# One tile's feed-forward steps begin at the tenth of sixteen packing groups, on a new layout of PSUM

## The chip, the cores and the metric

The kernel runs on one core of one Trainium2 chip. A core has TensorE (PE, matmuls into the accumulator memory PSUM, eight banks), VectorE (DVE), ScalarE (ACT), GpSimd (POOL), and SyncE (SP), which here issues most of the loads. The metric is the device time of one execution in microseconds.

## What is computed

Everything is f32. Packing attention takes 32 learned vectors per head over the keys and values; a second attention lets each token look at its head's 32 packed vectors; then come a dense feed-forward layer and a layer in which each token goes to one of eight experts.

```python
p_packed = sm_attn(p, k, v)                 # 8 batches, 8 heads, 32 x 576
x = sm_attn(q, p_packed, p_packed)          # 576 tokens per batch, head width 64
h = x @ w_in                                # 4608 x 512 -> 2048
g = where(h >= 1, h, where(h <= -1, 0, (h + 1)**2 / 4))
x = g @ w_out                               # -> 512
e = argmax(x @ w_gate); out = gate * (relu(x @ w1[e]) @ w2[e])
```

The kernel splits an f32 operand into a high and a low part and takes three matmuls per product: high by high, high by low, low by high.

## The kernel before

The work is in three parts: a packing stage, 12 tiles of tokens with 16 steps each, and 18 slots of expert work with a tail. Only the first two touch the change.

**Packing** goes over 16 groups (a batch and four of its heads). For a group, four score matmuls go into two banks of PSUM (`sc`, L413); VectorE takes the maximum over 576 keys (`nm`, L420, L421); ScalarE takes the exponential into the group's K buffer `kp` (L423); TensorE transposes the result in five blocks (L431 four into `tp`, L433 the last into the bank of `av`); ScalarE copies them out (L434 to L436); twenty small matmuls with V (L446) give `av`, which ScalarE scales into `packed` (L447). The score pool has two buffers, so a group's score may run before the last group's exponential is done. Three K buffers and three V buffers go round; they are the places of later weight tiles (`pw03`, `pw13`, `wo7`, and `pw02`, `pw12`, `wo6`).

**Weight units.** Beside the groups run 16 units of weights (four for each n = 0 to 3; two of them first-layer halves g, two second-layer). `load_unit` (L292) brings 1 MB of 64-bit numbers into a raw buffer that the table `RAW` names; the last four go into K buffers and the buffer `wr`. `prep_unit` (L303) makes two f32 parts of it: Abs on ScalarE (L315), four operations on VectorE (L316 to L319), a cast on ScalarE (L320), a subtraction on VectorE (L321). First-layer units are multiplied by the packed vectors into the weights that tile 0 needs: `first_product` (L338), 12 matmuls of 512 columns per (n, g), two casts and two subtractions of 128x512 (L351, L352). `spill` (L323) writes the unit to DRAM for the other tile pairs, which make their products by `product` (L354): three matmuls for each of four k, with casts and subtractions over 64 partitions each.

**Tile 0's attention** is four chains (`attn_chain`, L229) of a query load (SyncE, L237) and three pieces, hung to iterations of the packing loop by `soon`; tile 0 is of kind M: 512 columns from two batches, two pieces of 256. **A step** (`step`, L1012) is for one of 16 slices of the hidden width: 12 matmuls of 256 columns (`h`, L718), the activation on ScalarE and VectorE (L740 to L748), and 12 matmuls of 512 columns (L723 to L725) that add the slice of the step before to four `y` tiles. After the sixteenth the four are copied out (`yr`, L775).

**Order.** The program is written by one loop over the groups. A scheduler moves the instructions of TensorE, ScalarE, VectorE and GpSimd by their dependencies; SyncE's stay as written. `LEAD` (3) is how many steps are written in the packing loop, `at` hangs work to later steps. PSUM before: `h`, `a0`, `a1`, `y0`, one bank each, and the score pool of four, which is closed after the last group and becomes a second `h`, `a2`, `y1`, `y2` (the pool `late`).

Of the kernel before, what the change touches and what calls it, by code (L numbers as in the profile page):

```python
# [23 lines left out]
P = 128  # L24
# [14 lines left out]
LEAD = 3  # L39
# [45 lines left out]
def attn_moe_kernel(ctx, tc, qT, kT, vv, pT, wcat, wg, w2cat, out):  # L85
# [91 lines left out]
    def h_tile(G, name):  # L177
        if late and G % 2 and G >= 10:
            return late[0].tile([P, 512], F32, name=name, tag="h")
        return psm.tile([P, 512], F32, name=name, tag="h")  # L180
# [10 lines left out]
    n_y = [0]  # L191

    def y_tile(name):


        i = n_y[0] % 3 if late else 0
        n_y[0] = i + 1
        return (late[0] if i else psm).tile([P, 512], F32, name=name, tag=f"y{i}")
# [30 lines left out]
    def attn_chain(col0, b, ws, n, g, ah, al, pl, sfx):  # L229
# [5 lines left out]
        def load():  # L235
            qr = pl.tile([P, 2, SPLIT + HB], F32, name="qr" + sfx, tag="qr", bufs=2)
# [37 lines left out]
    def tile_chains(t, pl):  # L274
# [4 lines left out]
        for pi, (col0, b, ws, n) in enumerate(tile_pieces(t)):  # L279
            for g in range(2):  # L280
                r.append(attn_chain(col0, b, ws, n, g, ah, al, pl, f"_{t}_{pi}_{g}"))
# [8 lines left out]
    RAW = ["wo4", "wo5", "wr"] * 4 + ["pw03", "pw13", "wo7", "wr"]  # L290
# [47 lines left out]
    def first_product(n, g):  # L338


        if g == 0:
            products(0, n)
        for par in range(2):
            ps = a_tile([P, 512], f"pp0_{n}_{g}_{par}")
# [9 lines left out]
    def product(p, n, k):  # L354

        if k == 0:
            products(p, n)
        g, q = divmod(k, 2)
        ps = a_tile([P, 512], f"pp{p}_{n}_{k}")
        for i, (t, m) in enumerate(((0, 0), (0, 1), (1, 0))):  # L360
            pe.matmul(ps, lhsT=both(k, t), rhs=ws1[0][:, q, m, :], start=(i == 0), stop=(i == 2))
# [10 lines left out]
    def packing():  # L372
        p1_cm = tc.tile_pool(name="st1p", bufs=2, space=PSUM)
        p1 = p1_cm.__enter__()
        if True:
# [51 lines left out]
            def s1_tr(i):  # L427
                s = d[i]
                ps = a_tile([P, 512], f"tp{i}")
                for c in range(4):  # L430
                    pe.transpose(ps[:, c * P:(c + 1) * P], s["a1"][:, c * P:(c + 1) * P], ident)  # L431
                s["ps"] = a_tile([P, 512], f"av{i}")
                pe.transpose(s["ps"][:64, 256:384], s["a1"][:, 512:], ident)  # L433
                act.copy(s["tA"], ps[:, :384])  # L434
                act.copy(s["tB"][:, :P], ps[:, 384:])
                act.copy(s["tB"][:64, P:], s["ps"][:64, 256:384])  # L436
# [37 lines left out]
            for c, (load, pieces) in enumerate(tile_chains(0, st2)):  # L474
                soon(3 + 2 * c, load)
                for m in range(3):
                    soon(5 + 2 * c + m, pieces[m])
            for i in range(NG + 2):
                if i < NG:
                    s1_score(i)  # L480
                    s1_exp(i)
                if i == NG - 1:
                    p1_cm.__exit__(None, None, None)
                    late.append(ctx.enter_context(tc.tile_pool(name="late", bufs=1, space=PSUM)))
                if 0 <= i - 1 < NG:
                    s1_av(i - 1)
                if i < NG:
                    s1_tr(i)
# [6 lines left out]
                for u in range(-(-NU * i // NG), min(-(-NU * (i + 1) // NG), NU)):  # L495
# [3 lines left out]
                    if u % 4 < 2:  # L499
                        todo.append((u // 4, u % 4))  # L500
                if i >= 5 and todo and todo[0][0] < 2:
                    first_product(*todo[0])
                    spill(*todo.pop(0))
                if i == NG - 1:
                    for u in range(NU, FC):
# [606 lines left out]
```

## Time and profile before

| | us |
|---|---|
| median of three runs | 1249.33 (1248.11 to 1250.98) |
| the profiled execution | 1249.28 |
| its span | 1247.3 |
| first maximum of the packing starts | 10.6 |
| sixteenth maximum starts | 113.6 |
| last first-product subtraction starts | 162.08 |
| tile 0's results start to be copied out | 196.38 |

The page lists each engine's busy time over the whole span, and the views below cut it into stretches. A row of an engine in order of time gives the start, the duration, the line, the operation, output and input, and in brackets how long the engine had stood idle before and what ended the wait. Matmuls overlap: the distance between starts is what one costs, not its duration.

### The profile page before, as it was taken

What the parts mean: (1) busy time and instruction counts of PE and PEld (TensorE: products, weight loads), DVE (VectorE), ACT (ScalarE), POOL (GpSimd) and SP (SyncE); (2) the same over time, 40 slices, a digit from 0 to 9 for tenths busy, and PEclk for the clock granted to TensorE, in tenths of its full rate; (3) what the DMA queues carried; (4) which work ended last, traced back from release to release, by engine and by line L of the source; (5) the groups of instructions that cost most, each with busy time, mean ns of one, the idle gap of its engine ahead of it and who ended that gap; (6) DMA issues with size and microseconds to landing.
All of it is one profiled execution on the core that took longest, in us unless ns stands there. A gap on an engine that the chain in (4) does not pass through costs nothing. (4 is left out here: it accounts for less than half of the span.)

```text
span 1247.3 us, 21251 instructions
## 1 busy us (share of the span) xinstructions
PE 1193.9 (96%) x7234; PEld 995.3 (80%) x7234; DVE 944.6 (76%) x2222; ACT 730.0 (59%) x1430; POOL 325.5 (26%) x567
## 2 busy tenths in 40 slices
PE   5787999999999999999999999999999999999997
PEld 2455888778778887678888887788999999999996
DVE  8888867988895959977869679899766666666663
ACT  4666656667566556565565455655565555555653
POOL 3221116623741105731211265512101000010010
PEclk8988999999999999999999999999999999999999
DMA  9995780143211232111331000601212512111150
GB/s 347 370 328 176 283 245 22 43 142 126 68 47 62 68 113 101 50 44 35 108 126 45 28 18 35 186 18 50 78 36 68 170 44 60 35 54 49 34 178 21
DMA packets 70179, 128.18 MB, mean 103 GB/s; under 512 B 10281, under 2 KB 46633, under 8 KB 66864
## 3 DMA queue, kind: packets, MB, share of 16 engines
q1 hardware_dynamic: 56464, 97.33, 24.2%
q0 software_dynamic: 5840, 18.95, 4.1%
q10 hardware_dynamic: 7760, 10.49, 2.7%
q8 instruction: 59, 0.97, 0.3%
q14 instruction: 56, 0.46, 0.1%
HBM read 162.31 MB, written 31.77 MB: 156 GB/s over the span
## 5 line engine op out<-in xcount | busy, mean ns | idle before, releaser
L718 PE MATMUL h<-ah,pw 128*128 128x256 f32 (+1 forms) x1024 | 242.6, 302 | 8.2 <-DVE rt L742 8.0
L869 DVE TENSOR_TENSOR sw<-raw,sw 128x1024 fp32r<-128x1024 f32 (+1 forms) x152 | 180.9, 1209 | 77.9 <-ACT sw L867 77.8
L885 PEld LDWEIGHTS gh<-gx,sw 128*128 128x128 f32 x1728 | 227.1, 191 | 12.8
L885 PE MATMUL gh<-gx,sw 128*128 128x256 f32 x1728 | 230.5, 283 | 0.0
L723 PE MATMUL y<-wo,gh 128*128 128x512 f32 x576 | 229.9, 399 | 0.6 <-ACT kp L423 0.6
L724 PE MATMUL y<-wo,gh 128*128 128x512 f32 x576 | 228.5, 397 | 0.0
L547 DVE CUSTOM_DVE_ANT_0 jk<-yr,wgb 128x512 bf16<-128x512 f32 x288 | 219.1, 761 | 5.6 <-ACT yr L775 3.5
L718 PEld LDWEIGHTS h<-ah,pw 128*128 128x128 f32 x1024 | 176.5, 190 | 31.0 <-DVE rt L742 13.4
L867 ACT CAST sw<-raw 128x1024 fp32r<-128x1024 f32 (+1 forms) x160 | 156.5, 1004 | 59.1 <-PE gy L725 53.9
L725 PE MATMUL y<-wo,gl 128*128 128x512 f32 x576 | 186.3, 400 | 2.1 <-POOL gl L748 1.9
L740 ACT ACTIVATE rt<-h,half 128x320 f32<-128x320 f32 (+1 forms) x192 | 111.0, 580 | 102.6 <-PE h L718 86.2
L747 ACT CAST gh<-rt 128x512 fp32r<-128x512 f32 (+2 forms) x192 | 98.1, 512 | 96.6 <-DVE rt L742 59.1
L718 PE MATMUL h<-al,pw 128*128 128x256 f32 (+1 forms) x512 | 152.7, 298 | 0.0
L742 DVE SCALAR_TENSOR_TENSOR rt<-h,rt 128x320 f32<-128x320 f32 (+1 forms) x192 | 105.5, 551 | 51.1 <-ACT rt L741 46.3
L908 POOL DMA_INDIRECT out<-go,xm x37 | 36.8, 993 | 362.3 <-ACT go L907 303.1
L725 PEld LDWEIGHTS y<-wo,gl 128*128 128x128 f32 x576 | 105.8, 189 | 30.0 <-POOL gl L748 5.1
L723 PEld LDWEIGHTS y<-wo,gh 128*128 128x128 f32 x576 | 108.7, 189 | 23.3 <-issue 2.1
L724 PEld LDWEIGHTS y<-wo,gh 128*128 128x128 f32 x576 | 108.9, 189 | 18.7
L889 ACT ACTIVATE ggh<-gh 128x256 fp32r<-128x256 f32 x144 | 55.0, 382 | 109.5 <-PE gh L885 103.8
L724 PE MATMUL gy<-sw,ggh 128*128 128x512 f32 x288 | 113.9, 395 | 0.0
L723 PE MATMUL gy<-sw,ggh 128*128 128x512 f32 x288 | 113.8, 395 | 0.0
L748 DVE TENSOR_TENSOR gl<-rt,gh 128x512 fp32r<-128x512 f32 (+1 forms) x128 | 84.1, 658 | 25.3 <-ACT gh L747 21.2
(220 smaller groups left out, 1762.5 us busy)
## 6 DMA issues: line engine op xcount, KB each, us to landing
raw<-in_w2cat SPq DMA_DIRECT2D x76, 1024.0 KB
ws<-wsd SPq DMA_DIRECT2D x48, 512.0 KB
wr<-in_wcat SPq DMA_DIRECT2D x16, 1024.0 KB
kp<-in_kT SPq DMA_DIRECT2D x16, 576.0 KB
xb<-xs SPq DMA_DIRECT2D x72, 128.0 KB
vr<-in_vv SPq DMA_DIRECT2D x16, 512.0 KB
wsd<-ws SPq DMA_DIRECT2D x8, 1024.0 KB
qr<-in_qT ACTq DMA_DIRECT2D x16, 320.0 KB
```

The costliest lines, as they stand in the source:

```text
L547: dve.tensor_tensor_reduce(out=junk, in0=rows[j][:, :DM], in1=wgb[0][:, e, :], scale=1.0, scalar=0.0, op0=ALU.mult, op1=ALU.add, accum_out ...
L718: pe.matmul(ps[:, col0:col0 + n], lhsT=w[:, g, part, c], rhs=x[:, g, col0:col0 + n], start=(n_mm == 0), stop=(n_mm == 5))
L723: pe.matmul(y, lhsT=gh, rhs=wh, start=first, stop=False)
L724: pe.matmul(y, lhsT=gh, rhs=wl, start=False, stop=False)
L725: pe.matmul(y, lhsT=gl, rhs=wh, start=False, stop=last)
L740: act.activation(v, ps[:, :W], AF.Relu, bias=half, scale=0.5)
L742: dve.scalar_tensor_tensor(out=v, in0=ps[:, :W], scalar=1.0, in1=v, op0=ALU.max, op1=ALU.min)
L747: act.copy(gh[:, :n], vk[:, :n])
L748: (pool if k == "A" else dve).tensor_tensor(out=gl[:, :n], in0=vk[:, :n], in1=f32(gh[:, :n]), op=ALU.subtract)
L867: act.copy(w[:, n, 0], r)
L869: (pool if sid == 0 and i else dve).tensor_tensor(out=w[:, n, 1], in0=r, in1=f32(w[:, n, 0]), op=ALU.subtract)
L885: pe.matmul(ps[:, :SL], lhsT=first(sid, 4 * (fc // 4) + k, part)[:, c], rhs=rh[:, k, :], start=(n_mm == 0), stop=(n_mm == 3 * KD - 1))
```

## The change

`LEAD` becomes `STEP0` = 9: a step is written at the end of every iteration from the tenth on, so nine of them lie in the packing loop's 18 iterations in place of three. To have room for four `y` tiles from then on, the main pool holds `h`, `a0`, `a1` and three `y`, the score pool has one buffer of two banks, and `late` is a second `h` and `a2`. A group's transposes and `av` share one bank (`bank(...)`, always the first from the eleventh group on), and the last transposed block goes into spare columns of the group's own score tile. The query loads of tile 0's second piece go into buffers of the steps' activation (`spare`), and its chains are hung to earlier iterations. First products for n = 2 and 3 take `product`'s form (`product_of`). The last units: 12 is loaded at iteration 14, 13 at 15, 14 and 15 at 16, in place of all four at 15; their `RAW` names are reordered; preparation and late products are hung anew.

```diff
@@ -36,7 +36,7 @@
 EARLY = 8
 ROW = DM + 2
 NU = 12
-LEAD = 3
+STEP0 = 9
 OOB = 1 << 20
 SCALE = 1.0 / 8.0
 
@@ -175,7 +175,7 @@
     fourth = [None]
 
     def h_tile(G, name):
-        if late and G % 2 and G >= 10:
+        if late and G % 2:
             return late[0].tile([P, 512], F32, name=name, tag="h")
         return psm.tile([P, 512], F32, name=name, tag="h")
 
@@ -188,14 +188,8 @@
         return bank(use[n_a[0] % len(use)], shape, name)
 
 
-    n_y = [0]
-
     def y_tile(name):
-
-
-        i = n_y[0] % 3 if late else 0
-        n_y[0] = i + 1
-        return (late[0] if i else psm).tile([P, 512], F32, name=name, tag=f"y{i}")
+        return psm.tile([P, 512], F32, name=name, tag="y", bufs=3)
 
     def ps_tile(name):
         if not done:
@@ -226,14 +220,17 @@
         c = D * (par ^ (k % 2))
         return pk[:, k, part, c:c + P]
 
-    def attn_chain(col0, b, ws, n, g, ah, al, pl, sfx):
+    def attn_chain(col0, b, ws, n, g, ah, al, pl, sfx, spare=False):
 
 
         st = {}
         nb = n // 32
 
         def load():
-            qr = pl.tile([P, 2, SPLIT + HB], F32, name="qr" + sfx, tag="qr", bufs=2)
+            if spare:
+                qr = work.tile([P, 2, SPLIT], F32, name="qr" + sfx, tag="rt", bufs=2)
+            else:
+                qr = pl.tile([P, 2, SPLIT + HB], F32, name="qr" + sfx, tag="qr", bufs=2)
             (act if done else sp).dma_start(qr[:, :, :n], qT[b, 2 * g:2 * g + 2, :, ws:ws + n].rearrange("q p s -> p q s"))
             st["qr"] = qr
 
@@ -278,7 +275,7 @@
         r = []
         for pi, (col0, b, ws, n) in enumerate(tile_pieces(t)):
             for g in range(2):
-                r.append(attn_chain(col0, b, ws, n, g, ah, al, pl, f"_{t}_{pi}_{g}"))
+                r.append(attn_chain(col0, b, ws, n, g, ah, al, pl, f"_{t}_{pi}_{g}", t == 0 and pi == 1))
         return r
 
     def wtile(n, shape, dt, name):
@@ -287,7 +284,7 @@
 
     wout, wstage, wprod = {}, {}, {}
     wraw = {}
-    RAW = ["wo4", "wo5", "wr"] * 4 + ["pw03", "pw13", "wo7", "wr"]
+    RAW = ["wo4", "wo5", "wr"] * 4 + ["pw13", "wo7", "pw03", "wr"]
 
     def load_unit(u):
 
@@ -340,8 +337,12 @@
 
         if g == 0:
             products(0, n)
+        if n > 1:
+            for q in range(2):
+                product_of(0, n, 2 * g + q, wstage[2 * n + g][:, q])
+            return
         for par in range(2):
-            ps = a_tile([P, 512], f"pp0_{n}_{g}_{par}")
+            ps = ps_tile(f"pp0_{n}_{g}_{par}")
             i = 0
             for q in range(2):
                 for t, m in ((0, 0), (0, 1), (1, 0)):
@@ -355,10 +356,13 @@
 
         if k == 0:
             products(p, n)
+        product_of(p, n, k, ws1[0][:, k % 2])
+
+    def product_of(p, n, k, w):
         g, q = divmod(k, 2)
         ps = a_tile([P, 512], f"pp{p}_{n}_{k}")
         for i, (t, m) in enumerate(((0, 0), (0, 1), (1, 0))):
-            pe.matmul(ps, lhsT=both(k, t), rhs=ws1[0][:, q, m, :], start=(i == 0), stop=(i == 2))
+            pe.matmul(ps, lhsT=both(k, t), rhs=w[:, m, :], start=(i == 0), stop=(i == 2))
         for par in range(2):
             r = slice(D * (par ^ q), D * (par ^ q) + D)
             o = wprod[n][par]
@@ -370,7 +374,7 @@
     s1 = s1_cm.__enter__()
 
     def packing():
-        p1_cm = tc.tile_pool(name="st1p", bufs=2, space=PSUM)
+        p1_cm = tc.tile_pool(name="st1p", bufs=1, space=PSUM)
         p1 = p1_cm.__enter__()
         if True:
             NG = B * 2
@@ -426,14 +430,15 @@
 
             def s1_tr(i):
                 s = d[i]
-                ps = a_tile([P, 512], f"tp{i}")
+
+                ps = s["ps"] = bank(0 if i > STEP0 else i % 2, [P, 512], f"tp{i}")
                 for c in range(4):
                     pe.transpose(ps[:, c * P:(c + 1) * P], s["a1"][:, c * P:(c + 1) * P], ident)
-                s["ps"] = a_tile([P, 512], f"av{i}")
-                pe.transpose(s["ps"][:64, 256:384], s["a1"][:, 512:], ident)
+                last = s["sc"][:64, 0, 512 - P:]
+                pe.transpose(last, s["a1"][:, 512:], ident)
                 act.copy(s["tA"], ps[:, :384])
                 act.copy(s["tB"][:, :P], ps[:, 384:])
-                act.copy(s["tB"][:64, P:], s["ps"][:64, 256:384])
+                act.copy(s["tB"][:64, P:], last)
 
             def s1_av(i):
                 s = d[i]
@@ -472,43 +477,43 @@
                 soon(i + 2, lambda i=i: build_pk(i // 2, i % 2))
 
             for c, (load, pieces) in enumerate(tile_chains(0, st2)):
-                soon(3 + 2 * c, load)
+                soon(1 + c, load)
                 for m in range(3):
-                    soon(5 + 2 * c + m, pieces[m])
+                    soon(3 + c + m, pieces[m])
             for i in range(NG + 2):
                 if i < NG:
                     s1_score(i)
                     s1_exp(i)
+                if 0 < i <= STEP0 + 1:
+                    s1_av(i - 1)
+                if i < NG:
+                    s1_tr(i)
                 if i == NG - 1:
                     p1_cm.__exit__(None, None, None)
                     late.append(ctx.enter_context(tc.tile_pool(name="late", bufs=1, space=PSUM)))
-                if 0 <= i - 1 < NG:
-                    s1_av(i - 1)
-                if i < NG:
-                    s1_tr(i)
                 for fn in early.get(i, []):
                     fn()
                 if i + 3 < NG:
                     s1_load(i + 3)
                 if i + 2 < NG:
                     s1_load_v(i + 2)
-                for u in range(-(-NU * i // NG), min(-(-NU * (i + 1) // NG), NU)):
+                if STEP0 < i < NG:
+                    s1_av(i)
+                if i in (NG, NG + 1):
+                    late_product(2, i - NG)
+                for u in range(-(-NU * i // NG), -(-NU * (i + 1) // NG)) if i < NG else ((NU,), (NU + 1, NU + 2))[i - NG]:
                     prep_unit(u)
                     if 0 < u < NU - 2:
                         load_unit(u + 2)
-                    if u % 4 < 2:
+                    if u % 4 < 2 and u < 8:
                         todo.append((u // 4, u % 4))
-                if i >= 5 and todo and todo[0][0] < 2:
+                if i >= 5 and todo:
                     first_product(*todo[0])
                     spill(*todo.pop(0))
-                if i == NG - 1:
-                    for u in range(NU, FC):
-                        load_unit(u)
-                if i >= NG + 2 - LEAD:
+                for u in {NG - 2: (NU,), NG - 1: (NU + 1,), NG: (NU + 2, NU + 3)}.get(i, ()):
+                    load_unit(u)
+                if i >= STEP0:
                     step()
-            for n, g in todo:
-                first_product(n, g)
-                spill(n, g)
 
 
     wgb = []
@@ -1003,11 +1008,9 @@
         for m in range(4):
             at(b0 + (3, 5, 7, 9)[m], lambda nx=nx, m=m: split_w(nx, 0, m))
             at(b0 + 2 + 2 * m, lambda nx=nx, m=m: split_w(nx, 1, m))
-    def late_unit(u):
-        prep_unit(u)
-        if u % 4 < 2:
-            first_product(u // 4, u % 4)
-            spill(u // 4, u % 4)
+    def late_product(n, g):
+        first_product(n, g)
+        spill(n, g)
 
     def step():
         t, fc = divmod(len(done), FC)
@@ -1023,9 +1026,10 @@
         for fn in bg.pop(G, []):
             fn()
 
-    for u in range(NU, FC):
-        at(LEAD + u - NU, lambda u=u: late_unit(u))
-    at(LEAD + FC - NU, close_s1)
+    at(9, lambda: late_product(3, 0))
+    at(10, lambda: late_product(3, 1))
+    at(10, lambda: prep_unit(FC - 1))
+    at(11, close_s1)
     packing()
     while len(done) < GE:
         step()
```

In the rows of the queues, a name's number tells which tile it is; h_7 is step 7's, sc_1314, sc_1403 and sc_1489 are the scores of groups 13, 14 and 15.

TensorE before, from the score of group 14 (sc_1217) to that of group 15 (sc_1269) and on:

```order
L413 MATMUL sc_1217<-kp_195 64x288 x4
L723 MATMUL y_2_1393<-wo_387,gh_1337 128x512
L724 MATMUL y_2_1393<-wo_387,gh_1337 128x512
L446 MATMUL av_1197<-vr_1090 32x64 x20
L413 MATMUL sc_1269<-kp_191 64x288 x4
L725 MATMUL y_2_1393<-wo_387,gl_1338 128x512
L718 MATMUL h_2_1414<-ah_224,pw_0_0_623 128x256
```

TensorE in the changed kernel, from the score of group 14 to the first step after group 15:

```order
L417 MATMUL sc_1403<-kp_195 64x288 x4
L436 MATMUL tp_1415<-ident,kp_195 128x128 x4
L438 MATMUL sc_1403<-ident,kp_195 64x128
L451 MATMUL tp_1415<-vr_1243 32x64 x20
L417 MATMUL sc_1489<-kp_191 64x288 x4
L436 MATMUL tp_1501<-ident,kp_191 128x128 x4
L438 MATMUL sc_1489<-ident,kp_191 64x128
L451 MATMUL tp_1501<-vr_1335 32x64 x20
L365 MATMUL pp_2_1_1580<-ws_1077,pk 128x512 x3
L723 MATMUL h_7_1602<-ah_224,pw_1_0_822 128x256
```

The two groups stand with nothing between them; before, half a y and an h stood there.

ScalarE before, from the exponential of group 14 on (ca is a unit's Abs, wr_1157 unit 11's load):

```order
L423 ACTIVATE kp_195,rs_1225<-sc_1217,nm_1222 128x576
L315 ACTIVATE ca_1261<-wr_1157 128x1024
L740 ACTIVATE rt_1429<-h_2_1414,half 128x512
L423 ACTIVATE kp_191,rs_1277<-sc_1269,nm_1274 128x576
L434 COPY vr_1145<-tp_1250 128x384
L435 COPY vr_1145<-tp_1250 128x128
L436 COPY vr_1145<-av_1255 64x128
L741 ACTIVATE rt_1429<-rt_1429 128x512
L747 CAST gh_1427<-rt_1429 128x512
L320 CAST wo_1260<-ca_1261 128x2x512
L436 COPY vr_1205<-av_1311 64x128
L447 ACTIVATE packed<-av_1255,rs_1225 128x64
```

ScalarE in the changed kernel, from unit 11's Abs (wr_1276) through those of units 12 and 13 (wr_1454, wr_1535) to the exponential of group 15 (kp_191):

```order
L312 ACTIVATE ca_1446<-wr_1276 128x1024
L452 ACTIVATE packed<-tp_1326,rs_1322 128x64
L312 ACTIVATE ca_1590<-wr_1454 128x1024
L317 CAST wo_1445<-ca_1446 128x2x512
L427 ACTIVATE kp_195,rs_1411<-sc_1403,nm_1408 128x576
L439 COPY vr_1243<-tp_1415 128x384
L440 COPY vr_1243<-tp_1415 128x128
L441 COPY vr_1243<-sc_1403 64x128
L452 ACTIVATE packed<-tp_1415,rs_1411 128x64
L312 ACTIVATE ca_1653<-wr_1535 128x1024
L427 ACTIVATE kp_191,rs_1497<-sc_1489,nm_1494 128x576
L439 COPY vr_1335<-tp_1501 128x384
```

The Abs of units 12 and 13 now stand ahead of the exponentials of groups 14 and 15; before, no Abs of a unit after 11 did.

SyncE before, at the last loads of the packing (vr is V, wr a unit, wsd the spill):

```order
L405 DMA vr_1145<-in_vv 64x256
L300 DMA wr_1157<-in_wcat 128x2048
L404 DMA vr_1205<-in_vv 128x4x256
L405 DMA vr_1205<-in_vv 64x256
L300 DMA wr_1316<-in_wcat 128x2048
L300 DMA wr_1318<-in_wcat 128x2048
L300 DMA wr_1320<-in_wcat 128x2048
```

SyncE in the changed kernel, at the same place:

```order
L409 DMA vr_1243<-in_vv 64x256
L297 DMA wr_1276<-in_wcat 128x2048
L408 DMA vr_1335<-in_vv 128x4x256
L409 DMA vr_1335<-in_vv 64x256
L297 DMA wr_1454<-in_wcat 128x2048
L297 DMA wr_1535<-in_wcat 128x2048
L321 DMA wsd<-ws_1077 128x2048
L297 DMA wr_1598<-in_wcat 128x2048
L297 DMA wr_1600<-in_wcat 128x2048
```

Unit 12's load now stands with unit 13's ahead of a spill, and the last two behind it; before, four stood in a row.

## Rows read from the trace of the kernel before

**Rows 1.** The page's part 1: engines' busy us, share of the span, instructions.
```profile
PE 1193.9 (96%) x7234; PEld 995.3 (80%) x7234; DVE 944.6 (76%) x2222; ACT 730.0 (59%) x1430; POOL 325.5 (26%) x567
```

**Rows 2.** Busy time by stretch: length, engines' us (instructions), TensorE's clock, DMA share, GB/s.
```profile
core 0: us, PE busy (x) PEld busy (x) DVE busy (x) ACT busy (x) POOL busy (x), PEclk, DMA share, GB/s
0.00:10.60 10.60, 2.19 (x8) 0.86 (x8) 6.30 (x20) 2.61 (x3) 9.41 (x83) 1.00 0.85 297
10.60:92.00 81.40, 62.13 (x689) 36.34 (x693) 68.50 (x136) 51.13 (x133) 16.47 (x33) 0.85 1.00 354
92.00:107.00 15.00, 8.30 (x106) 5.52 (x107) 12.65 (x24) 9.44 (x20) 3.58 (x5) 0.73 1.06 353
107.00:132.50 25.50, 24.92 (x243) 19.28 (x242) 16.63 (x26) 15.73 (x32) 0.00 (x0) 0.96 0.29 102
132.50:162.70 30.20, 30.20 (x162) 24.71 (x160) 29.04 (x41) 19.29 (x31) 3.43 (x3) 1.00 0.85 307
162.70:196.40 33.70, 33.70 (x187) 28.23 (x184) 16.33 (x31) 17.38 (x33) 6.03 (x12) 1.00 0.56 169
196.40:1247.00 1050.60, 1032.45 (x5853) 880.32 (x5851) 795.19 (x1950) 614.43 (x1185) 286.57 (x434) 1.00 0.22 70
```

**Rows 3.** ScalarE in order of time at 196.4: start, duration, line, operation, output and input.
```profile
196.38 2.04 ACT L775 COPY yr<-y 128x512 f32<-128x512 f32 x4
```

**Rows 4.** VectorE in order of time, 152 to 169.
```profile
152.13 0.68 DVE L352 TENSOR_TENSOR pw<-pp,pw 128x512 fp32r<-128x512 f32 x1
152.73 1.21 DVE L319 SCALAR_TENSOR_TENSOR ca<-wr,ca 128x1024 int32<-128x1024 int32 x1
...
162.08 0.69 DVE L352 TENSOR_TENSOR pw<-pp,pw 128x512 fp32r<-128x512 f32 x1 [0.53 <-ACT pw L351]
...
168.30 0.52 DVE L249 STREAM_TRANSPOSE qr<-s 128x320 f32<-128x320 f32 x1
```

**Rows 5.** TensorE in order of time, 162.9 to 167.5: one step.
```profile
162.98 0.39 PE L718 MATMUL h<-ah,pw 128*128 128x256 f32 x1
...
164.52 0.39 PE L723 MATMUL y<-wo,gh 128*128 128x512 f32 x1
...
167.41 0.76 PE L247 MATMUL s<-qr,pkf 128*64 128x320 f32 x4
```

**Rows 6.** ScalarE in order of time: a group's work, and two late units' Abs.
```profile
84.41 0.48 ACT L434 COPY vr<-tp 128x384 f32<-128x384 f32 x1 [0.17 <-PE tp L431]
...
86.33 0.76 ACT L423 ACTIVATE kp<-sc,nm 128x576 f32<-128x576 f32 x1
...
86.97 0.21 ACT L423 ACTIVATION_READ_ACCUMULATOR kp<-sc,nm 128x1 f32 x1
...
131.40 1.12 ACT L315 ACTIVATE ca<-wr 128x1024 f32<-128x1024 f32 x1 [0.57 <-DMA wr<-in_wcat]
...
133.86 1.16 ACT L315 ACTIVATE ca<-wr 128x1024 f32<-128x1024 f32 x1 [0.65 <-DMA wr<-in_wcat]
```

**Rows 7.** TensorE in order of time: transposes and score at two clocks.
```profile
87.23 0.66 PE L431 MATMUL tp<-ident,kp 128*128 128x128 f32 x4
...
90.81 1.19 PE L413 MATMUL sc<-kp 128*64 128x288 f32 x8
...
97.08 1.11 PE L431 MATMUL tp<-ident,kp 128*128 128x128 f32 x4 [4.25 <-ACT kp L423]
...
99.12 2.19 PE L413 MATMUL sc<-kp 128*64 128x288 f32 x8
```

**Rows 8.** One line's instructions: the maximum of each group.
```profile
L420 DVE TENSOR_REDUCE nm<-sc x16: 737/751/759, 10.6 to 113.6; 128x1 f32<-128x576 f32 x16
```

**Rows 9.** SyncE's queue in order of time, 126.5.
```profile
126.56 2.13 SPq L300 DMA_DIRECT2D wr<-in_wcat  x4
```

**Rows 10.** SyncE's waits, 0 to 200: line, what it waited for, us, times, longest.
```profile
SPq L300 <- PE tp L431: 22.0, 1, 22.0
...
SPq L237 <- POOL al L268: 10.4, 1, 10.4
```


## The prediction, made before the changed kernel was run

> **What bounds the kernel now.** I read the page's first part, then the busy time by stretch, then instructions in order of time. TensorE is busy 96% of the span [rows 1], so over the whole program its work is the limit. The stretches [rows 2] show where that is not so: TensorE idles 8.41, 19.27 and 6.70 us in the first three, 0.58 in the fourth, and nothing from 132.5 to 196.4, where tile 0 ends (the four copies of its result start at 196.38 [rows 3]). All of the edit lies ahead of that point, and behind it the same steps run in the same order at 98% TensorE. So the change in tile 0's end is the change in the kernel, and the question is how much of the 35.0 us idle is filled, and whether new idle time opens.
>
> TensorE works 161.4 us up to there (the six busy times of [rows 2]). VectorE, which prepares the weights, is busy 68.50 of 81.40 us, 12.65 of 15.00, 16.63 of 25.50 and 29.04 of 30.20: it idles 12.90, 2.35, 8.87 and 1.16, together 25.3 us, up to the last subtraction of a first product (162.08 [rows 4]). It is therefore nearly as full as TensorE, and what counts is its idle time ahead of that subtraction.
>
> **The change part by part.**
>
> *Nine steps in the packing instead of three.* A step costs TensorE 1.54 us for h (162.98 to 164.52) and 2.89 for y (164.52 to 167.41) [rows 5]; six more are 26.6 us. In the written order they all lie beside groups 9 to 15, but the reordered queue shows steps up to the sixth beside groups 9 to 12, and none beside 13 to 15. There TensorE has one group's score, transposes and products after the other's: h of step 7 stands behind score 15, since its bank opens only when the score pool closes.
>
> *The products for n = 2, 3 in the other form.* TensorE loses 24 matmuls of 512 columns, at the 0.24 us that y's twelve of that size take each (2.89 / 12 [rows 5]): 5.8 us. VectorE gets 16 subtractions of half the partitions in place of 8 whole ones. The duration goes by the columns, 512 in both, so I price each at the 0.60 that one takes to the next start (152.13 to 152.73 [rows 4]): 4.8 us more. From both sides: no row shows a subtraction over 64 partitions with 512 columns; at half the price the 16 cost what the 8 did, nothing, and at 0.69 [rows 4] they cost 5.5. ScalarE has eight more casts, which lie beside VectorE's.
>
> *One score buffer; the last transposed block in its bank.* Score i+1 now waits for group i's maximum, exponential, transposes and three copies; behind the waiting score on TensorE stand the next group's transposes, and VectorE's maximum waits for it. The loop is: copies, the longest 0.48 [rows 6], about 1.0 together; score 1.19 [rows 7]; maximum 0.75 [rows 8]; exponential with its accumulator read 0.97 [rows 6]; transposes 0.66 [rows 7] and a small one: 4.8, and with a hand-over of some 0.2 at each of five places (0.17 before the copy of [rows 6]) about 6 us. Before, fully laden groups came every 6.87 us (maxima from 10.6 to 113.6, 15 intervals [rows 8]). So by itself the single buffer costs nothing; it takes away the slack.
>
> *Loads of the late units.* This is the dear part. Unit 12's load goes into the K buffer of group 13 and unit 13's into that of group 14, so each is issued when that group's transposes are done. ScalarE's Abs of these units, which waits for the load, stands in the queue ahead of exponentials 14 and 15: while it waits, the packed copy, the exponential and with them transposes, copies and the next score stand still. The price is in the trace: the four late loads were issued at 126.56, and Abs of the first started at 131.40, 4.84 us on, having waited for the transfer; the second at 133.86, 2.46 later [rows 6, 9]. The wait that held these loads, 22.0 us on a group's transposes [rows 10], cost little before, as the Abs stood behind the last exponential. Now the loop from one group's transposes to the next's is 4.84 + 1.12 (Abs) + 0.97 + 0.66 = 7.6 us for groups 14 to 15. For 13 to 14 a V load and unit 11's megabyte are ahead in the queue, priced as one more megabyte, 2.46: 10.1. From 12 to 13 no load is waited for: 6. Together 23.7; VectorE's maxima stand behind pieces of unit work of up to 1.22 us [rows 4], so up to 27.3; I take 25.
>
> Between maxima 12 and 15 VectorE has unit 11, four of unit 12's five pieces and three maxima, some 13 us by the distances of [rows 4]. It idles 25 - 13 = 12 us there.
>
> *Units 8 and 10* are asked for by ScalarE in the same way, ahead of exponentials. Each may wait up to a full 4.84 [rows 6, 9], or nothing if the load is early enough; VectorE has other steps' work beside them. I take 1 us each.
>
> *The second piece's query loads* no longer wait in SyncE's queue (10.4 us [rows 10]). In this stretch every transfer was ahead of its user and the DMA share is 1.00 [rows 2]; nothing to nothing, or a microsecond off units 8 and 10.
>
> **The sum.** VectorE's work ahead of the last first-product subtraction was 126.8 us from 10.6 on (four rows of [rows 2]). Added: products 4.8; the last unit's final subtraction 1.1 (152.73 is a like piece [rows 4], less its overlap); two operations of three more steps, 3.6 at 0.60 each; one more attention chain, six small instructions of at most 0.52 [rows 4], about 2.0. That is 11.5. After that subtraction TensorE still owes h of steps 12 to 15 and y of 11 to 15: 4 x 1.54 + 5 x 2.89 = 20.6. So tile 0 ends at 10.6 + 126.8 + 11.5 + 20.6 = 169.5 plus VectorE's idle time. Break-even is 196.4 - 169.5 = 26.9 us idle, where before it was 25.3: the change can hardly afford any. I expect 12.90 + 2.35 as before in the earlier groups, 2 for units 8 and 10, 12 in groups 12 to 15, and 2 in the products that follow (1.16 before): 31.3. Tile 0 ends at 200.8, 4.4 us late. Before, the other side of the ledger hid this: TensorE had its own 161.4 us of work as limit; now it has 155.6 and waits.
>
> The profiled execution took 1249.28 (span 1247.3 and 2.0 around), as good as the median of 1249.33: 1249.3 + 4.4 = 1253.7. By the uncertain terms (loop 23.7 to 27.3, units 8 and 10 at 0 to 5, products 0 to 5.5) this case spans about 1249.5 to 1260.
>
> **The rivals.**
>
> *A. The loads are in time, and it is faster.* If the loads of units 11 to 13 land before ScalarE reaches them, since the groups run later than I think or the queue is emptier, the three loops are 6 us each: idle there 18 - 13 = 5, in all 12.90 + 2.35 + 5 + 1.2 = 21.5, tile 0 ends at 191.0, 5.4 early: 1243.9. For it: in the fourth stretch the DMA share was 0.29 [rows 2], so the queue has room. Against it: the buffers come free only with the groups' own transposes, so an earlier issue isn't to be had. It decides where the load lands within the 3 us or so between the transposes and the moment the next exponential could start.
>
> *B. Nothing to be measured.* Half of the waits of the forecast come true, idle about 27: within 0.2%, 1249.3. The two accounts, TensorE's gain of 5.8 and filled idle time against VectorE's 11.5 and the loop, cancel.
>
> *C. TensorE at its lower clock in groups 12 to 15.* In the third stretch TensorE was busy 8.30 of 15.00 us and the granted clock was 0.73 [rows 2]; a score took 2.19 us there against 1.19, a set of transposes 1.11 against 0.66 [rows 7]. Groups 13 to 15 would leave TensorE as sparse as that: 1.00 + 0.45 in each of four loops, 5.8 us on the path: 1253.7 + 5.8 = 1259.5. Against it: in the fourth stretch the clock was 0.96 with groups in it, but there the steps filled it.
> The Trainium skill has a rule that speaks for C ("TensorE: Matmul & The Clock Gate", Part 1): the gate passes all or half of the 2.4 GHz pulses by how busy the array has lately been. The trace agrees as far as 0.73 in the sparse stretch and 1.00 in the full ones go [rows 2]; by the rule the sum would be C's, by the rows of full stretches the forecast's.
>
> **How the numbers follow.** The forecast has a chance of 0.47, A 0.24, B 0.17, C 0.12. What a measurement can tell from no change is about 0.2%, 2.5 us. Faster by more than that is A, less a little that stays within: 0.23. Same is B and the near ends of A and of the forecast: 0.19. The rest, 0.58, is slower. The range goes from A's 1243.9 to a little above C, 1263; the likeliest case's own is 1249.5 to 1260.
>
> **What would show it.** In the new trace: ScalarE's Abs waits for the DMA two or three times before the last exponential, by 2 us or more each; maxima 12 to 15 come 7 to 10 us apart (6 under A); TensorE idles some 10 us between scores 13 and 15 and its granted clock there is near 1 (0.7 or so under C); the 16 half-height subtractions last about 0.6 us each; TensorE's idle time before the twelfth group is shorter than before, and tile 0's copies start near 201. Copies that start before 194 would make the forecast wrong, as would a main part behind tile 0 that has changed by more than 2 us.

## The result, and the profile after

The changed kernel takes 1267.85 us (median of four runs, 1265.53 to 1268.39) against 1249.31: ratio 1.0149, 95% interval 1.0136 to 1.0161. The prediction had the direction, most of the place, and a fourth of the size: 4.4 us forecast, 18.5 measured. The profiled execution is the fastest of the four (1265.53, span 1263.7, so 16.4 over the span before).

The busy time by stretch, of the changed kernel (columns as in [rows 2]; the bounds are the tenth group's start, the last groups, the products, tile 0's end and tile 11's end):

```profile
10.70:85.00 74.30, 59.78 (x560) 38.43 (x561) 64.23 (x129) 48.68 (x124) 17.34 (x29) 0.82 0.98 344
85.00:119.00 34.00, 33.11 (x329) 24.17 (x328) 27.22 (x48) 22.59 (x44) 5.13 (x11) 1.00 0.60 209
119.00:149.50 30.50, 13.60 (x208) 8.32 (x207) 15.43 (x25) 10.65 (x26) 0.10 (x1) 0.73 0.62 194
149.50:175.00 25.50, 17.39 (x78) 13.95 (x79) 20.97 (x27) 17.81 (x28) 0.00 (x0) 0.83 0.82 292
175.00:188.25 13.25, 13.25 (x60) 10.53 (x60) 8.31 (x15) 6.52 (x11) 2.89 (x3) 0.90 1.04 311
188.25:209.90 21.65, 21.01 (x118) 17.64 (x117) 10.19 (x19) 10.23 (x19) 2.92 (x5) 1.00 0.21 71
209.90:837.30 627.40, 617.75 (x3230) 505.35 (x3230) 505.91 (x1439) 381.94 (x840) 241.80 (x393) 1.00 0.23 73
837.30:1263.70 426.40, 419.25 (x2631) 376.09 (x2629) 284.63 (x512) 233.89 (x350) 41.07 (x44) 1.00 0.22 64
```

From 85 to 119 the change does what it says: TensorE is busy 33.11 of 34.00 us. Before, over the same time, it was busy 25.44:

```profile
85.00:119.00 34.00, 25.44 (x308) 17.39 (x309) 29.17 (x51) 22.17 (x51) 4.69 (x6) 0.85 0.75 253
```

Then it idles 16.9 us in the last groups and 8.1 in the products. Tile 0's copies start 13.5 us later than at [rows 3]:

```profile
209.92 0.59 ACT L780 COPY yr<-y 128x512 f32<-128x512 f32 x1 [0.63 <-PE y L730]
```

The experts take 426.4 us, as before (426.5, from tile 11's copies at 820.8 to the span's end); tiles 1 to 11 take 627.4 in place of 624.4.

In the last groups, ScalarE of the changed kernel in order of time (L312 is a unit's Abs, L317 its cast, L427 the exponential):

```profile
127.01 1.12 ACT L312 ACTIVATE ca<-wr 128x1024 f32<-128x1024 f32 x1 [2.27 <-DMA wr<-in_wcat]
...
132.16 1.15 ACT L312 ACTIVATE ca<-wr 128x1024 f32<-128x1024 f32 x1 [3.82 <-DMA wr<-in_wcat]
133.19 1.05 ACT L317 CAST wo<-ca 128x1024 fp32r<-128x1024 f32 x1
134.12 0.76 ACT L427 ACTIVATE kp<-sc,nm 128x576 f32<-128x576 f32 x1
...
143.15 1.12 ACT L312 ACTIVATE ca<-wr 128x1024 f32<-128x1024 f32 x1 [4.38 <-DMA wr<-in_wcat]
145.15 0.74 ACT L427 ACTIVATE kp<-sc,nm 128x576 f32<-128x576 f32 x1 [0.88 <-DVE nm L425]
```

Three Abs, of units 11, 12 and 13, wait for their loads ahead of exponentials 14 and 15. TensorE there, transposes (L436) and scores (L417):

```profile
123.25 0.66 PE L436 MATMUL tp<-ident,kp 128*128 128x128 f32 x4 [1.16 <-ACT kp L427]
...
125.47 1.19 PE L417 MATMUL sc<-kp 128*64 128x288 f32 x8
135.02 1.11 PE L436 MATMUL tp<-ident,kp 128*128 128x128 f32 x4 [8.36 <-ACT kp L427]
...
138.25 2.06 PE L417 MATMUL sc<-kp 128*64 128x288 f32 x8
146.03 1.12 PE L436 MATMUL tp<-ident,kp 128*128 128x128 f32 x4 [5.71 <-ACT kp L427]
```

The transposes are those of groups 13, 14 and 15. The loops, from one group's transposes to the next's, take 11.8 and 11.0 us. TensorE waits 8.36 and 5.71 of them for the exponential, and from 135 on its matmuls have the durations that [rows 7] has for the lower clock (granted 0.73 over the stretch from 119). SyncE's queue has the loads of units 11 (119.67), 12 and 13 (the second of the pair went out at 136.83, after group 14's transposes) and the last two:

```profile
119.67 0.54 SPq L297 DMA_DIRECT2D wr<-in_wcat  x1
...
124.16 12.67 SPq L297 DMA_DIRECT2D wr<-in_wcat  x2
...
147.51 0.80 SPq L297 DMA_DIRECT2D wr<-in_wcat  x2
```

### The profile page after: what moved, and what is told of

Same layout as the page of the kernel before. It is cut to its first block, busy times and chain, and to the rows that moved or that the text cites. A ratio compares the mean times of both kernels' runs of the same rounds, so it can differ in the third digit from the quotient of the medians.

```text
span 1263.7 us, 21251 instructions
## 1 busy us (share of the span) xinstructions
PE 1197.3 (95%) x7210; PEld 995.3 (79%) x7210; DVE 943.2 (75%) x2230; ACT 734.9 (58%) x1438; POOL 320.7 (25%) x567
## 5 line engine op out<-in xcount | busy, mean ns | idle before, releaser
L723 PE MATMUL h<-ah,pw 128*128 128x256 f32 (+1 forms) x1024 | 245.6, 304 | 13.8 <-DVE rt L747 10.2
L552 DVE CUSTOM_DVE_ANT_0 jk<-yr,wgb 128x512 bf16<-128x512 f32 x288 | 214.2, 744 | 5.1 <-ACT yr L780 3.0
L730 PE MATMUL y<-wo,gl 128*128 128x512 f32 x576 | 188.9, 401 | 2.2 <-POOL gl L753 2.1
L747 DVE SCALAR_TENSOR_TENSOR rt<-h,rt 128x320 f32<-128x320 f32 (+1 forms) x192 | 105.4, 550 | 44.0 <-ACT rt L746 41.7
L729 PEld LDWEIGHTS y<-wo,gh 128*128 128x128 f32 x576 | 109.2, 189 | 18.5
L723 PEld LDWEIGHTS h<-al,pw 128*128 128x128 f32 x512 | 98.2, 192 | 7.5 <-issue 1.0
```

Source lines behind the costliest of these rows:

```text
L552: dve.tensor_tensor_reduce(out=junk, in0=rows[j][:, :DM], in1=wgb[0][:, e, :], scale=1.0, scalar=0.0, op0=ALU.mult, op1=ALU.add, accum_out ...
L723: pe.matmul(ps[:, col0:col0 + n], lhsT=w[:, g, part, c], rhs=x[:, g, col0:col0 + n], start=(n_mm == 0), stop=(n_mm == 5))
L729: pe.matmul(y, lhsT=gh, rhs=wl, start=False, stop=False)
L730: pe.matmul(y, lhsT=gl, rhs=wh, start=False, stop=last)
L747: dve.scalar_tensor_tensor(out=v, in0=ps[:, :W], scalar=1.0, in1=v, op0=ALU.max, op1=ALU.min)
```

## The experiments

Tile 0's end is the start of its copies in each run's profile, which is one execution. In e13 and e6, whose times lie within about 0.1% of the kernel before, it lies 1.2 us later and 0.4 earlier, so a difference of about a microsecond there says little. Of the edits, only the lines that matter are shown.

| run | us | ratio to before, 95% | tile 0's end |
|---|---|---|---|
| before | 1249.31 | | 196.38 |
| the change | 1267.85 | 1.0149 (1.0136 to 1.0161) | 209.92 |
| e1 loads as before | 1274.48 | 1.0193 (1.0178 to 1.0208) | 219.31 |
| e2 no loads 12, 13 | 1266.51 | 1.0136 (1.0120 to 1.0151) | 211.49 |
| e4 new form alone | 1255.09 | 1.0047 (1.0032 to 1.0061) | 202.17 |
| e5 change, old form | 1261.91 | 1.0104 (1.0088 to 1.0119) | 203.07 |
| e8 no loads 11 to 13 | 1253.18 | 1.0028 (1.0014 to 1.0042) | 205.63 |
| e10 e8, old form | 1247.64 | 0.9984 (0.9973 to 0.9994) | 198.63 |
| e3 steps from 15 | 1283.10 | 1.0261 (1.0243 to 1.0280) | 229.03 |
| e3b steps from 12 | 1274.46 | 1.0193 (1.0175 to 1.0211) | 220.28 |
| e11 e5, unit 11 early | 1258.93 | 1.0081 (1.0067 to 1.0095) | 202.04 |
| e12 e11, Abs held | 1255.81 | 1.0048 (1.0034 to 1.0061) | 199.09 |
| e13 one score buffer alone | 1249.40 | 1.0004 (0.9995 to 1.0013) | 197.59 |
| e16 e4, half the subtractions | 1246.49 | 0.9985 (0.9976 to 0.9994) | 194.28 |
| e17 e4, GpSimd subtracts | 1255.13 | 1.0053 (1.0040 to 1.0067) | 203.01 |
| e6 chains alone | 1250.23 | 1.0011 (1.0002 to 1.0020) | 195.96 |

**Which wait.** My theory was the one in the prediction, that the Abs of units 12 and 13 hold up exponentials 14 and 15; its rival, that bare groups with one score buffer are slow by themselves.

```diff
 e1, on the changed kernel
-    RAW = ... + ["pw13", "wo7", "pw03", "wr"]
+    RAW = ... + ["pw03", "pw13", "wo7", "wr"]
-    for u in {NG - 2: (NU,), NG - 1: (NU + 1,), NG: (NU + 2, NU + 3)}.get(i, ()):
+    for u in range(NU, FC) if i == NG - 1 else ():
 e2, on the changed kernel, in the same loop
+    if u < NU + 2: wraw[u] = raw11[0]
+    else: load_unit(u)
```

> The changed kernel with one part undone: units 12 to 15 are loaded in the order and at the iteration of the kernel before, so that their Abs stand behind the last exponential. Theory 1 (the loss is ScalarE's Abs waiting for units 12 and 13 ahead of exponentials 14 and 15, 3.8 and 4.4 us, and the lower clock that follows): the two loops become 6 to 9 us in place of 11.7 and 11.0, some 8 us are won there and part is given back because units 12 and 13 are prepared later: 1258 to 1263. Theory 2 (the loss is the single score buffer and the bare groups, whatever ScalarE waits for): 1266 to 1269.

> The changed kernel without the loads of units 12 and 13; their preparation reads unit 11's raw data again, so that part of the weights is not the reference's. Everything else is as in the changed kernel. Theory 1: the waits of 3.8 and 4.4 us are gone, as well as some of the time at the lower clock: 8 to 12 us less than the changed kernel, 1256 to 1260, still slower than before. Theory 2: 1265 to 1269.

Both missed: e1 is slower than the change, and e2 is 1.3 us faster where 8 to 12 were expected, with tile 0's end 1.6 us later. For exponential 15 the theory holds: the loop from group 14 to 15, 11.0 us in the change, takes 7.4 in e1 and 7.8 in e2. TensorE of e2, transposes of these two groups:

```profile
136.57 1.12 PE L439 MATMUL tp<-ident,kp 128*128 128x128 f32 x4 [9.42 <-ACT kp L430]
...
144.34 1.11 PE L439 MATMUL tp<-ident,kp 128*128 128x128 f32 x4 [1.97 <-ACT kp L430]
```

But the loop from 13 to 14, 11.8 us in the change, takes 12.0 and 12.8 with no load of unit 12 ahead of it. ScalarE of e2 says why (L315 is the Abs, L320 the cast, L430 the exponential):

```profile
127.99 2.15 ACT L315 ACTIVATE ca<-wr 128x1024 f32<-128x1024 f32 x2 [2.77 <-DMA wr<-in_wcat]
130.03 0.31 ACT L455 ACTIVATE packed<-tp,rs 128x64 f32<-128x64 f32 x1
134.74 1.05 ACT L320 CAST wo<-ca 128x1024 fp32r<-128x1024 f32 x1 [4.39 <-DVE ca L319]
135.69 0.73 ACT L430 ACTIVATE kp<-sc,nm 128x576 f32<-128x576 f32 x1
```

Exponential 14 starts at 135.69, even later than in the change: ahead of it stand unit 11's Abs, which waits for its load, and unit 11's cast, which waits for VectorE's four operations on that Abs. The wait for unit 12 had merely run beside that. In e1 the loads of units 12 to 15 went out at 145.95 together, behind group 15, and VectorE had little to do before: it was busy 9.1 us from 119 to 149.5, 15.4 in the change. In e2 the groups end 1.7 us earlier than in the change (144.34, 146.03), and more than that is lost behind them: TensorE is busy 58.0 us from there to tile 0's end, 54.6 in the change; why is open. The theory fell as to the unit that holds exponential 14; the next runs left unit 11's load out too, with the new form and without it.

```diff
 e8, on the changed kernel (e10: the same on e5)
+    if u == NU - 1:
+        wraw[u] = raw8[0]      # load_unit
+        return
+    if u < NU + 2: wraw[u] = raw8[0]
+    else: load_unit(u)
 e5, on the changed kernel
-        if n > 1:
-            for q in range(2):
-                product_of(0, n, 2 * g + q, wstage[2 * n + g][:, q])
-            return
```

> The changed kernel without the loads of units 11, 12 and 13; their preparation reads unit 8's raw data again, so those weights are not the reference's. Their Abs, and unit 11's cast, now stand ahead of exponential 12 or beside it, and nothing of them between exponentials 13 and 15. Theory 1, amended (exponential 14 waits for unit 11: its load, its Abs, its four operations on VectorE and its cast, some 9 us in all; units 12 and 13 only follow): the maxima of groups 13 to 15 come 6 to 7 us apart, and 6 to 10 us are won: 1258 to 1262. Theory 2 (groups that stand alone on TensorE with one score buffer are slow by themselves): maxima 10 us apart, 1265 to 1268.

> The kernel of the run before this one (no loads of units 11 to 13), with the first products for n = 2 and 3 in the old form as well. Theory 1, amended, together with the form's price of 6 us: the two add up, 1252 to 1256. Theory 2: 1259 to 1262, as the changed kernel with the old form.

> The changed kernel with the first products for n = 2 and 3 in the form of before. If the form helps TensorE in its last stretch, where it is full: 1270 to 1274. If the form is part of the loss (eight more casts and subtractions in the stretch after the groups, where TensorE waits for them): 1262 to 1266.

The times of e8 and e10 must not be read as they stand, nor against what was expected of them: with other weights other tokens can go to other experts, and from tile 11's end their spans last 418.0 and 418.7 us where the change has 426.4 (e2 and e16, which leave out less, have 426.4 and 426.9). By tile 0's end the late loads are worth 4.3 us (209.92 to 205.63) with the new form and 4.4 (203.07 to 198.63) without; the form 6.9 or 7.0. The form was expected to help by 2 to 6 or to cost 2 to 6: it costs. Two runs with all data loaded followed:

```diff
 e11, on e5
+                if i == 11:
+                    load_unit(11)      # ahead of s1_load(i + 3)
 e12, on e11
-        act.activation(f32(ca), f32(high), AF.Abs)
+        act.activation(f32(ca), f32(high), AF.Abs, bias=hold[0] if u in (12, 13) else 0.0)
+    hold[0] = nm * 0.0      # one VectorE operation behind group 15's maximum
```

> The changed kernel with the old form of the first products, and unit 11's load written one iteration earlier, ahead of that iteration's K and V loads, with all loads kept. Unit 11's Abs and cast now stand ahead of exponential 12, units 12 and 13's Abs still ahead of 14 and 15. Amended theory (unit 11 first, units 12 and 13 behind it): the loop from 13 to 14 falls from some 11.7 to 7.6 or 8.5 us, that to 15 from 11.0 to about 7.6; against 1261.9 with the old form alone this makes 1255 to 1259. If the gain of the run without loads came only from transfers left out: 1260 to 1263.

> The same with the Abs of units 12 and 13 held behind group 15's maximum (by a zero bias that is computed from it), so that nothing stands ahead of exponentials 13 to 15; all loads kept. If waiting on ScalarE is the cost: loops of 6 to 6.5 us, and 1249 to 1254. If VectorE's work, now later, takes it back: 1256 to 1259, like the run before this one.

e11 wins 1.0 us at tile 0's end and 3.0 in time, at the edge of what was expected: its loop from 13 to 14 falls to 8.0 us, as expected, and that from 14 to 15 stays at 10.9, where 7.6 was expected. e12 wins 2.9 and 3.1 more, and its time lies between its two expectations; its groups end 5.9 us earlier than e5's (transposes of group 15 at 141.37 and 147.25), and 1.9 of that is given back behind them. Together that is 4.0 of the 4.4 at tile 0's end, so the waits on ScalarE, not the transfers left out, were the price. In e12 nothing stands ahead of the last exponentials, and TensorE's transposes (L436) and scores (L414) still read:

```profile
121.26 0.60 PE L436 MATMUL tp<-ident,kp 128*128 128x128 f32 x4
...
126.59 1.11 PE L436 MATMUL tp<-ident,kp 128*128 128x128 f32 x4 [1.98 <-ACT kp L427]
...
129.82 2.19 PE L414 MATMUL sc<-kp 128*64 128x288 f32 x8
133.98 1.12 PE L436 MATMUL tp<-ident,kp 128*128 128x128 f32 x4 [1.98 <-ACT kp L427]
...
141.37 1.11 PE L436 MATMUL tp<-ident,kp 128*128 128x128 f32 x4 [1.97 <-ACT kp L427]
```

The first two loops as stretches (columns as in [rows 2]):

```profile
121.26:126.59 5.33, 2.73 (x54) 1.57 (x52) 1.94 (x8) 2.40 (x7) 1.59 (x2) 0.99 0.32 105
126.59:133.98 7.39, 4.89 (x53) 2.68 (x54) 1.23 (x5) 1.94 (x6) 0.00 (x0) 0.50 0.59 193
```

The first loop takes 5.33 us at a granted clock of 0.99 (2.4 GHz), with TensorE busy 2.73 of it; the next two take 7.39 each at 0.50 (1.2 GHz). Behind the first bare loop the clock is at its lower level, and TensorE's own work makes the loop 2.1 us longer. This is rival C, which had 1.45 a loop for it, and no run took it away.

**The form.**

```diff
 e4, on the kernel before, in first_product
+        if n > 1:
+            for q in range(2):
+                product_of(0, n, 2 * g + q, wstage[2 * n + g][:, q])
+            return
 e16, on e4, in product_of
+            if p == 0 and par == 1:
+                pool.memset(f32(o[r, g, 1, :]), 0.0)
+                continue
 e17, on e4, in prep_unit
-        dve.tensor_tensor(out=lo, in0=f32(ca), in1=f32(hi), op=ALU.subtract)
+        (pool if u >= NU else dve).tensor_tensor(out=lo, in0=f32(ca), in1=f32(hi), op=ALU.subtract)
```

> The kernel before with one part of the change alone: the first products for n = 2 and 3 in the other form. If VectorE is nearly as full as TensorE there, as the prediction has it, its 4.8 us of added work takes back most of TensorE's 5.8: 1246 to 1251. If TensorE alone is the limit there: 1243.5.

> The kernel before with the new form for n = 2 and 3, and with eight of its sixteen subtractions left out (GpSimd writes zeros there, so half of those low parts are missing from the result). If VectorE's added work is the form's price: tile 0 ends 2 to 6 us before that of the kernel before (196.4) and the time is 1243 to 1247. If it is the casts on ScalarE and the hand-overs of smaller pieces: tile 0 ends at 200 to 202, 1252 to 1255.

> The kernel before with the new form, and with the last subtraction of units 12 to 15 (1.2 us each on VectorE) on GpSimd, which is idle there: all of the result is computed. VectorE has then as much work as before. If VectorE's added work is the price and GpSimd is quick enough: 1243 to 1249. If GpSimd's subtraction takes several microseconds and stands ahead of the products, or if the price is elsewhere: 1252 to 1258.

Alone on the kernel before the form costs 6 us, outside what I expected. Its sixteen subtractions on VectorE, over 100 to 203 us:

```profile
L373 DVE TENSOR_TENSOR pw<-pp,pw 64x512 fp32r<-64x512 f32 x16 | 10.9, 686 | 0.3
```

Half the partitions take as long as all of them did (0.686 us, 0.68 at [rows 4]). TensorE and VectorE from 132.5 to 162.7, in e4 and then in e16:

```profile
132.50:162.70 30.20, 24.53 (x129) 19.38 (x127) 29.76 (x42) 21.58 (x33) 5.07 (x3) 0.99 0.67 253
```

```profile
132.50:162.70 30.20, 28.11 (x149) 22.08 (x148) 29.46 (x41) 24.33 (x38) 6.30 (x7) 1.00 0.90 330
```

VectorE is full in both. In e4 TensorE idles 5.7 us of the stretch that it filled before [rows 2]; with eight subtractions fewer it idles 2.1, and tile 0 ends 7.9 us earlier, 2.1 ahead of the kernel before. So the form's price lies in VectorE's subtractions and not in the casts, which e16 keeps. Whether it is their time on a full engine or their place behind each product, e16 can't tell apart, since it takes away both. e17 was to do so by giving other work of VectorE away, and could not: GpSimd took 2.4 to 3.3 us for what VectorE does in 1.2, and some of VectorE's own rows lengthened:

```profile
144.03 3.31 POOL L321 TENSOR_TENSOR ws<-ca,ws 128x1024 fp32r<-128x1024 f32 x1 [2.04 <-ACT ws L320]
...
152.82 2.41 POOL L321 TENSOR_TENSOR ws<-ca,ws 128x1024 fp32r<-128x1024 f32 x1 [3.93 <-ACT ws L320]
```

```profile
L317 DVE TENSOR_SCALAR ca<-ca 128x1024 int32<-128x1024 int32 x6 | 6.1, 1020 | 0.1
```

(from 0.752 us in e4 over the same stretch). In the changed kernel the form bites between 149.5 and 175. e8, which has it, and then e10, which differs by it alone:

```profile
149.50:175.00 25.50, 17.12 (x84) 13.37 (x83) 23.71 (x31) 19.00 (x28) 0.00 (x0) 0.87 0.85 282
```

```profile
149.50:175.00 25.50, 25.50 (x138) 20.62 (x138) 23.55 (x32) 18.32 (x29) 1.58 (x1) 1.00 0.94 307
```

TensorE idles 8.4 us with the new form and not at all with the old. What it waits for there in the changed kernel, most first (e8 has the same two at 4.6 and 2.2):

```profile
PE h L723 <- DVE rt L747: 4.6, 1, 4.6
PE h L723 <- DVE pw L370: 2.2, 2, 1.3
```

The longest wait is not for a product but for a step's activation (L747), which stands in VectorE's queue among subtractions and unit work.

**Layout, steps, chains.**

```diff
 e3 (e3b: 12), on the changed kernel
-STEP0 = 9
+STEP0 = 15
 e13, on the kernel before
-        p1_cm = tc.tile_pool(name="st1p", bufs=2, space=PSUM)
+        p1_cm = tc.tile_pool(name="st1p", bufs=1, space=PSUM)
 e6, on the kernel before: attn_chain and tile_chains as changed, and
+                soon(1 + c, load)
+                    soon(3 + c + m, pieces[m])
```

> The changed kernel with the steps written from iteration 15 on, three of them in the packing loop as before; layout, loads, chains and form as in the changed kernel. If the layout and the late loads are the loss whatever the number of steps: 1264 to 1268. If the loss beside the form's 6 us comes from TensorE's steps being used up before groups 13 to 15: 1254 to 1258.

> The same with the steps from iteration 12 on, six of them in the packing loop: between the changed kernel and the one with steps from 15 on under either theory; under the first 1264 to 1268, under the second 1258 to 1263.

> The kernel before with one buffer for the scores in place of two, and nothing else changed. By the prediction a loop of 6 us under groups every 6.87 us costs nothing, or one or two: 1249 to 1252. If the second buffer was what let a group's score run while VectorE and ScalarE were behind: 1255 to 1265.

> The kernel before with tile 0's chains hung earlier and the second piece's query loads in the activation's buffers, alone. By the prediction the 10.4 us wait on SyncE was hidden: nothing, 1248 to 1251. If earlier loads or chains take up time of VectorE ahead of the groups: 1251 to 1254; if the K and V loads behind that wait were late: 1244 to 1248.

One score buffer alone costs nothing that can be told, nor do the chains alone (e6's 0.1% lies within what I called no change, and its tile 0 ends 0.4 us earlier). e3 and e3b missed on the slow side of both theories: in the new layout, with its late loads, each three steps taken out of the packing put tile 0's end off by about 9 to 10 us (209.92, 220.28, 229.03). (`STEP0` also sets from which group on the products with V are written in the group's own iteration, and the bank of its transposes, so these two move with the steps.) With three steps in the packing, as before, tile 0 thus ends 32.7 us later than in the kernel before; the earlier steps win back 19.1 of that, and had to pay for the rest.

## Why the prediction was wrong in size

The sum was 10.6 + 126.8 + 11.5 of VectorE's work, 31.3 of its idle time, 20.6 of TensorE's tail: 200.8. The new profile, with the last first-product subtraction ending at 189.96, has 10.7, 137.8 of work, 41.4 idle and 20.0: 209.9. Work and tail were right within a microsecond. The term that failed is the idle time. VectorE of the changed kernel, cut at the sum's own bounds, maximum 12 (114.60) and maximum 15 (140.37), and at 149.5:

```profile
10.70:114.60 103.90, 88.49 (x831) 59.25 (x832) 89.14 (x169) 68.87 (x160) 20.68 (x37) 0.87 0.88 309
114.60:140.37 25.77, 15.05 (x218) 9.53 (x216) 13.01 (x26) 10.20 (x26) 1.89 (x4) 0.80 0.62 189
140.37:149.50 9.13, 2.94 (x46) 2.15 (x47) 4.74 (x8) 2.85 (x7) 0.00 (x0) 0.67 0.54 180
```

- Up to maximum 12: 17.3 idle expected (12.90 + 2.35 + 2), 14.8 measured.
- Maxima 12 to 15: 25 us with 12 idle expected, 25.8 with 12.8 measured. The total is right, partly by luck. Of the loops, priced at 6, 10.1 and 7.6, the first took 3.7, the others 11.8 and 11.0. The 13-to-14 loop was priced by unit 12's load, but by e1 and e2 it is unit 11's load, Abs, VectorE work and cast that hold exponential 14; I saw the cast in the queue and did not price it. In the 14-to-15 loop, unit 13's Abs started 6.3 us after its load went out (136.83 to 143.15), in place of 4.84. The load went out 1.8 us after the transposes had begun, which ran at the lower clock, and exponential 15 waited another 0.88 for the small operation behind its maximum (L425), which stood on VectorE behind unit 13's first operation:

```profile
144.30 0.69 DVE L313 TENSOR_SCALAR ca<-ca 128x1024 f32<-128x1024 f32 x1 [3.17 <-ACT ca L312]
144.91 0.15 DVE L425 TENSOR_SCALAR nm<-nm 128x1 f32<-128x1 f32 x1
```

- "2 in the products that follow": 13.9 measured from maximum 15 on (4.4 up to 149.5, then 4.5, 4.9 and 0.1 to 189.96). This is the step that failed, the largest miss. First, the loops were priced from transposes to transposes and the idle time counted from maximum to maximum, so the wait ahead of exponential 15 (3.17 above) fell out of the sum. Then VectorE waits for the first products, which TensorE starts at 149.27 at the lower clock. And I counted the new form's 4.8 us as added work for VectorE, and then let VectorE run through it at 96%. It is full only from 155 to 178; TensorE, which waits for it, idles there (8.4 us in e8, none in e10, which differs by the form alone), falls behind with its steps, and from 175 on is itself the limit, with VectorE idle. The two engines took turns at being full.
- The lower clock of rival C came with the waits, where the forecast had it as a case of its own: TensorE is busy 160.3 us up to tile 0's end, where the sum had 155.6.
- Behind tile 0: nothing expected, 3.0 us measured in tiles 1 to 11, and another 2.3 us between the profiled execution and the median. The premise that all of the edit lies ahead of tile 0's end was wrong: the layout of PSUM stays for every tile. Tiles 1 to 11 last 622.0 to 624.4 us in all runs of the old layout and 625.5 to 627.9 in all of the new; e5, e11 and e12 also have some 2.5 us more in the experts (428.9 to 429.2). Which instruction it is stays open.

Of the forecast's signs, the waits of the Abs came, and the maxima 9.5 and 9.6 us apart (6.7 for the first pair). The granted clock of 0.73 is rival C's sign, and tiles 1 to 11 grew by more than the 2 us allowed.

The single buffer (nothing), the query loads (nothing) and the direction were right. Rival A's premise was half met by e12, loads that hold up nothing, with the old form. It did not bring tile 0's end 5 us forward but 2.7 back: its three loops took 20.1 us where A had 18, and behind them TensorE was full (56.3 of 57.7 us), so hardly any idle time was left to win there. At tile 0's end the 13.5 us are 6.9 for the form, 4.4 for the late loads, and 2.2 left in e10. There TensorE idles 34.4 us up to tile 0's end (35.0 before) and is busy 164.2 (161.4), with 1377 matmuls to 1383: what the early steps fill, the bare groups open again, and what is left are matmuls that take longer. The clock granted in e10 from 119 to 149.5 is 0.78, which fits; that it is the whole of the 2.2 is not shown.

The Trainium skill ("TensorE: Matmul & The Clock Gate", Part 1) has the gate follow how busy the array has lately been; the trace agrees, 1.00 in the stretch that steps filled and 0.73 in the one after.

No version here is shown to beat the kernel before: e10 and e16 come in below it by less than 0.2%, and both leave work out.

## What to carry to other kernels

When two engines are both nearly full, price a change that moves work from one to the other on both: here 5.8 us off TensorE and 4.8 onto VectorE cost 6, and the price shows as turn-taking, idle time on each in turn. Idle time that is summed between two marks needs every wait of the chain between the same marks. A wait at the head of an in-order queue is priced with all that stands behind it there, and the first instruction of a unit that waits brings its later ones along (here the cast behind four VectorE operations). And before a run that leaves data out is read by its time, look whether the data steer the rest of the program.

## What the runs showed of the hardware

- A VectorE subtraction from PSUM takes 0.686 us over 64 partitions with 512 columns (e4), and 0.684 over 128 (the kernel before).
- With GpSimd doing subtractions of 128x1024 beside it (2.4 to 3.3 us each), VectorE's shift-and-mask of that size went from 0.752 (e4) to 1.020 us (e17) on average; the cause was not isolated.
- Between two bare groups of the same instructions, the loop took 5.33 us at a granted clock of 0.99 and 7.39 at 0.50 (e12).
